# Attention followed by a mixture of adapters: the mixture steps of most batches placed one head pair later, and one batch's x transposed on TensorE

## The chip, the cores and the metric

The kernel runs on one core of a Trainium2 chip, in one launch. The metric is the device time in microseconds: 240.66 us is the median of 3 runs (239.62 to 241.18).

## The reference

Eight batches of T5-style attention (8 heads, 576 positions, 64 features a head), then a mixture of rank-16 adapters over all 4608 rows of 512 features. Shortened:

```
scores = q @ k.T / sqrt(64) + bias_table[bucket(|i - j|)]      # per batch and head
attn   = softmax(scores);  x = concat over heads of attn @ v   # x: 4608 x 512
logits = x @ w_gate                                            # 8 experts
w      = softmax over the two largest logits of a row
out    = x + sum over these two e of w_e * (x @ A[e]) @ B[e]
```

## The kernel before

All matmuls take bf16 operands. A **pair** is two heads of one batch; 8 batches of 4 pairs make 32 pairs, and a pair i has five steps g = 0 to 4, so n = 5 i + g counts 160 steps. In each step TensorE computes the scores of the next step (`qk(n + 1)`), ScalarE takes the exponential of this one (`expo(n)`, L350, 128x1024 elements), and VectorE multiplies the bias band into the one before (`band`). Steps 1 to 3 of a pair also multiply the probabilities of the pair before with v (`pv`, L380); VectorE divides by the row sums and so writes x (`recip`, `norm`). Step 0 transposes q and k of the next pair on TensorE (`transposes`, L297; copy kqT on VectorE). The first 512 positions of a batch go in tiles of 128; the last 64 positions of every two batches share one tile, the tail.

**The mixture** of batch b runs spread over the pairs of the batches behind it. The function `mixture(b)` puts each of its parts into the table `events` with `at_slot(di, g, ...)`: pair 4 (b + 1) + di, step g. The parts are, in the order in which they depend on one another: `m_xdma` (L432), a DMA that SyncE issues and that transposes the four 128-row tiles of x into xT, 16 blocks of 128x128, inside the core's memory; or `m_x`, which does the same with 16 transposes on TensorE into PSUM (two tiles `xps` of 8 blocks, L443) and two copies on VectorE, and which only the last batch uses; `m_xtail`, the tail's part of xT, for odd b; `m_logits` (L465), 16 or 20 matmuls from xT, a copy and the row maxima on VectorE, a subtraction on GpSimd; `m_gate`, an exponential on ScalarE and small operations on GpSimd and VectorE that make the gate; `m_z` (L511), 16 or 20 matmuls from xT, multiplied by the gate on VectorE; `m_zT`, transposes of z and a copy; `m_out` (L532, L542), for each of the four row tiles a matmul and an addition of x on VectorE, and after the second and the fourth tile four output stores that SyncE issues; `m_outt` (L547 to L557), the same for the tail.

**What sets the order.** The program is written out in order by hand. Every engine works through its own instructions in the order of the program and waits for what it needs; semaphores between engines come from the data. In one step the attention's parts are issued first and the step's `events` behind them. SyncE issues, in program order, the loads of q, k and v, the transpositions of x and the output stores; it is free to run ahead of the other engines until an instruction must wait. At step 0 of a batch's first pair stand the k and q loads of the next batch (`load_kq`, L106, 1 MB each) and eight loads of v (`load_v`, L114, 64 KB each); four more loads of v stand at step 0 of the second pair and four at step 0 of the third. GpSimd casts q, k (L147) and v (L152) to bf16 ahead of their use; the cast of v for a pair stands at the last step of the pair before it.

**Buffers.** x has four buffers, xT two, the loaded q, k and v two, the output tile o three. PSUM has two buffers for scores and four for all else (tag "acc").

Of the kernel before, what the change touches and what calls it, by code (L numbers as in the profile page):

```python
# [27 lines left out]
def kernel(  # L28
# [15 lines left out]
    B, H, S, D = q.shape  # L44
# [148 lines left out]
    for bv, lo, hi in runs[nsm:]:  # L193
        n = hi - lo
# [367 lines left out]
    def mixture(b):  # L562
        tail = b % 2 == 1
        i0 = HP * (b + 1)

        def at_slot(di, g, f, *a):
            events.setdefault(5 * (i0 + di) + g, []).append((f, a))

        if b < B - 1:
            at_slot(0, 4, m_xdma, b)  # L570
        else:
            at_slot(0, 4, m_x, b, 0)
            at_slot(0, 4, m_x, b, 1)
        if tail:
            at_slot(1, 4, m_xtail, b)
        at_slot(2, 0, m_logits, b)
        for n in range(4):
            at_slot(2, (2, 3, 4, 4)[n], m_gate, b, n)
        at_slot(3, 0, m_z, b, 0, 4)
        if tail:  # L580
            at_slot(3, 2, m_z, b, 4, 5)
        at_slot(3, 4, m_zT, b)
        at_slot(4, 0, m_out, b, 0)
        at_slot(4, 2, m_out, b, 1)
        at_slot(5, 0, m_out, b, 2)
        at_slot(5, 2, m_out, b, 3)
        if tail:
            at_slot(6, 4, m_outt, b)


    NPAIR = B * HP
# [1 line left out]
    for b in range(B):  # L593
        mixture(b)
    transposes(0)
    qk(0)
    for n in range(NG + 5):
        i, g = divmod(n, 5)
        b, hp = divmod(i, HP)
# [96 lines left out]
```

## Time and profile before

| | |
|---|---|
| median of 3 runs | 240.66 us (239.62 to 241.18) |
| profiled execution: span on the core, from the first to the last instruction | 235.5 us (its whole time is not given beside it) |
| TensorE busy | 178.6 us (76%), granted clock 0.915 on average |
| VectorE busy | 185.3 us (79%) |
| ScalarE busy | 160.7 us (68%), of it 153.3 us in the 160 exponentials |
| GpSimd busy | 101.2 us (43%) |
| DMA | 41.54 MB, mean 176 GB/s |

The profile is one execution. Busy times are sums over the whole span, with a start in which loads and the bias tables come in, and an end in which only the mixture of the last two batches is left. In it, L82 is a helper through which every VectorE instruction goes, so that VectorE's work is told apart by its tiles. PE is TensorE, PEld its weight load, DVE VectorE, ACT ScalarE, POOL GpSimd, SP SyncE; a q behind the name means the engine's queue (here: where it issues a DMA). PEclk is the granted share of TensorE's full clock.

### The profile page before, as it was taken

How to read it: one execution, taken by the hardware profiler on the slowest of the kernel's cores; microseconds unless marked ns; L12 is line 12 of the kernel's file. 1: busy time of each engine (PE TensorE's matmuls, PEld its weight loads, DVE VectorE, ACT ScalarE, POOL GpSimd, SP SyncE). 2: the span in 40 equal slices, each digit the busy share in tenths (PEclk: the TensorE clock that was granted, in tenths of full speed). 3: DMA queues.
4: the chain of work that ended last, by engine and by line, in shares of the span. 5: the costliest groups of instructions: out<-in, count | busy, mean ns of one | idle time of the engine just before them, and what ended most of it. 6: DMA issues, size and time to landing. Idle time of an engine off the chain costs nothing.

```text
span 235.5 us, 6536 instructions
## 1 busy us (share of the span) xinstructions
PE 178.6 (76%) x2485; PEld 120.5 (51%) x2496; DVE 185.3 (79%) x540; ACT 160.7 (68%) x180; POOL 101.2 (43%) x195
## 2 busy tenths in 40 slices
PE   0177749886999898869992799989892999986560
PEld 0034426554765665546661576566561766665420
DVE  6329648893999999949895389999993799998770
ACT  0368637994899799936993379988990789892000
POOL 8440797562455455534453144554551543220100
PEclk9998997997999999979997589999996799999957
DMA  6977999999978979964998899896998603810616
GB/s 170 197 177 209 346 154 213 260 143 183 330 95 171 190 206 268 207 146 83 268 190 186 182 263 202 184 180 124 332 153 188 133 0 85 187 42 8 180 38 185
DMA packets 91831, 41.54 MB, mean 176 GB/s; under 512 B 69648, under 2 KB 87192, under 8 KB 91800
## 3 DMA queue, kind: packets, MB, share of 16 engines
q1 hardware_dynamic: 71720, 38.75, 70.0%
q0 software_dynamic: 17888, 1.85, 15.4%
q10 hardware_dynamic: 2192, 0.53, 1.4%
q8 instruction: 19, 0.31, 0.6%
q14 instruction: 12, 0.10, 0.1%
HBM read 29.84 MB, written 9.45 MB: 167 GB/s over the span
## 4 chain that ended last, share of the span: by engine, by line
DVE 37%; PE 28%; DMA 20%; issue 4%; ACT 4%; SPq 2%; POOL 2%; POOLq 0%; DVEq 0%
DVE p L82 12%; DMA xT<-x 12%; PE pv L380 10%; DVE x L82 7%; PE sc L334 7%; DVE o L82 4%; ACT p L350 4%; DMA tl<-in_q_dram 2%; DVE rc L82 2%; DMA vf<-in_v_dram 2%; PE tps L306 2%; PE kqps L297 2%; DMA qf<-in_q_dram 2%; DVE kqT L82 2%; PE zp L511 2%
## 5 line engine op out<-in xcount | busy, mean ns | idle before, releaser
L350 ACT ACTIVATE p<-sc 128x1024 bf16<-128x1024 f32 x160 | 153.3, 1034 | 39.8 <-PE sc L334 30.7
L82 DVE TENSOR_TENSOR p<-p,M 128x512 bf16<-128x512 bf16 (+2 forms) x160 | 73.6, 475 | 0.0
L380 PE MATMUL pv<-vn,p 128*128 128x65 bf16 (+1 forms) x1152 | 62.7, 203 | 1.7 <-DVE p L82 1.7
L380 PEld LDWEIGHTS <-p 128*128 128x128 bf16 x1280 | 53.9, 102 | 12.1 <-issue 11.2
L334 PE MATMUL sc<-kqT 64*128 64x512 bf16 x256 | 52.7, 411 | 8.1 <-ACT p L350 5.2
L147 POOL CAST kqn<-qf 128x512 bf16<-128x512 f32 x29 | 17.8, 613 | 35.5 <-DVE rc L82 33.7
L297 PE MATMUL kqps<-ident,kqn 128*128 128x128 bf16 x256 | 21.6, 230 | 14.2 <-DVE kqn L82 7.9
L152 POOL CAST vn<-vf 128x512 bf16<-128x512 f32 x28 | 17.3, 620 | 30.8 <-DVE p L82 15.7
L380 PE MATMUL pv<-vt,p 128*128 128x130 bf16 x128 | 29.0, 227 | 0.0
L82 DVE COPY kqT<-kqps 128x1024 bf16<-128x1024 bf16 x32 | 21.9, 683 | 8.7 <-PE kqps L297 8.6
L297 PEld LDWEIGHTS <-kqn 128*128 128x128 bf16 x256 | 15.5, 102 | 23.0 <-DVE kqn L82 8.2
L334 PEld LDWEIGHTS <-kqT 64*128 64x128 bf16 x256 | 12.9, 94 | 24.2 <-issue 14.7
L82 DVE TENSOR_TENSOR o<-dl,x 128x512 f32<-128x512 f32 x32 | 21.4, 680 | 1.0 <-PE dl L532 0.7
L147 POOL CAST kqn<-kf 128x512 bf16<-128x512 f32 x29 | 18.0, 622 | 7.3 <-DVE p L82 6.3
L465 PE MATMUL lp<-Wb,xT 128*128 128x8 bf16 x144 | 5.1, 167 | 18.2 <-DMA xT<-x 17.0
L82 DVE TENSOR_TENSOR x<-pv,rc 128x384 bf16<-128x384 f32 x32 | 17.8, 557 | 1.1
L82 DVE RECIPROCAL rc<-pv 128x6 f32<-128x6 f32 x64 | 11.7, 182 | 4.3 <-PE pv L380 4.0
L465 PEld LDWEIGHTS <-xT 128*128 128x128 bf16 x144 | 4.4, 99 | 19.6 <-DMA xT<-x 18.1
L475 POOL TENSOR_TENSOR df<-lg,m 128x32 f32<-128x32 f32 (+1 forms) x8 | 2.1, 261 | 27.8 <-DVE m L82 27.8
L343 PEld LDWEIGHTS <-kqT 128*128 128x128 bf16 x128 | 10.2, 101 | 7.4 <-issue 3.0
L82 DVE COPY tlT<-tps 128x1024 bf16<-128x1024 bf16 x8 | 5.5, 690 | 10.3 <-PE tps L306 10.2
L82 DVE TENSOR_TENSOR x<-pv,rm 128x256 bf16<-128x256 f32 x32 | 13.3, 417 | 0.0
(79 smaller groups left out, 209.4 us busy)
## 6 DMA issues: line engine op xcount, KB each, us to landing
out_dram<-o SPq DMA_DIRECT2D x64, 128.0 KB, 2.4
vf<-in_v_dram SPq DMA_DIRECT2D x120, 64.0 KB, 3.9
kf<-in_k_dram SPq DMA_DIRECT2D x7, 1024.0 KB, 6.4
qf<-in_q_dram SPq DMA_DIRECT2D x7, 1024.0 KB, 10.5
kf<-in_k_dram SPq DMA_DIRECT2D x4, 256.0 KB, 3.2
qf<-in_q_dram SPq DMA_DIRECT2D x4, 256.0 KB, 3.7
out_dram<-ot SPq DMA_DIRECT2D x8, 128.0 KB, 2.3
vf<-in_v_dram ACTq DMA_DIRECT2D x8, 64.0 KB, 4.5
```

Of the source, the lines that this page charges most:

```text
L82: self.last = f(*a, **kw)
L147: return (eng or nc.gpsimd).tensor_copy(o, s)
L152: return (eng or nc.gpsimd).tensor_copy(vns[b % 2][:, :, h, :D], vfs[b][:, :, h, :])
L297: nc.tensor.transpose(o[:, :, j, :], n[:, w, j], ident)
L306: nc.tensor.transpose(ps[:, w, c, :], tls[b % 2][:, w, c, :], ident)
L334: nc.tensor.matmul(sc[:, h * 512:(h + 1) * 512], lhsT=t[s, 0, g * 128:(g + 1) * 128], rhs=t[s, 1, :], start=True, stop=True)
L343: nc.tensor.matmul(sc[:, o:o + 128], lhsT=t[:, 0, j * 128:(j + 1) * 128], rhs=tt[:, 1, hp, :], start=True, stop=True, skip_group_check=True)
L350: nc.scalar.activation(p, scs.pop(n), ACT.Exp, scale=scale)
L380: nc.tensor.matmul(acc[:, k, o:o + n], lhsT=lhsT, rhs=rhs, start=start, stop=stop, skip_group_check=True)
L465: nc.tensor.matmul(lp[:, t, :], lhsT=xT[:, 4 * t + c, :], rhs=Wb[:, c, :], start=first, stop=(c == 3), skip_group_check=True)
L475: nc.gpsimd.tensor_tensor(df, lg, m8[:, :, 0:1].to_broadcast((128, nt, E)), op=ALU.subtract)
L511: nc.tensor.matmul(zp[:, t - t0, :], lhsT=xT[:, 4 * t + c, :], rhs=Ab[:, c, :], start=(t == t0 and c == 0), stop=(c == 3), skip_group_chec ...
```

## The change

For batches 0 to 5 everything from `m_logits` on moves to one pair later (d = 3 in place of 2); the transposition by DMA and the tail's part of xT stay where they are. Batch 6 is transposed by `m_x` on TensorE, at the step where its DMA stood; its other parts, and all of batch 7, stay where they are. No function is new.

```diff
--- before.py
+++ after.py
@@ -566,26 +566,27 @@
         def at_slot(di, g, f, *a):
             events.setdefault(5 * (i0 + di) + g, []).append((f, a))
 
-        if b < B - 1:
+        if b < B - 2:
             at_slot(0, 4, m_xdma, b)
         else:
             at_slot(0, 4, m_x, b, 0)
             at_slot(0, 4, m_x, b, 1)
         if tail:
             at_slot(1, 4, m_xtail, b)
-        at_slot(2, 0, m_logits, b)
+        d = 3 if b < B - 2 else 2
+        at_slot(d, 0, m_logits, b)
         for n in range(4):
-            at_slot(2, (2, 3, 4, 4)[n], m_gate, b, n)
-        at_slot(3, 0, m_z, b, 0, 4)
+            at_slot(d, (2, 3, 4, 4)[n], m_gate, b, n)
+        at_slot(d + 1, 0, m_z, b, 0, 4)
         if tail:
-            at_slot(3, 2, m_z, b, 4, 5)
-        at_slot(3, 4, m_zT, b)
-        at_slot(4, 0, m_out, b, 0)
-        at_slot(4, 2, m_out, b, 1)
-        at_slot(5, 0, m_out, b, 2)
-        at_slot(5, 2, m_out, b, 3)
+            at_slot(d + 1, 2, m_z, b, 4, 5)
+        at_slot(d + 1, 4, m_zT, b)
+        at_slot(d + 2, 0, m_out, b, 0)
+        at_slot(d + 2, 2, m_out, b, 1)
+        at_slot(d + 3, 0, m_out, b, 2)
+        at_slot(d + 3, 2, m_out, b, 3)
         if tail:
-            at_slot(6, 4, m_outt, b)
+            at_slot(d + 4, 4, m_outt, b)
 
 
     NPAIR = B * HP
```

In a batch, with the first pair called 0: before, pair 0 had the first two outputs of the batch two before and, at step 4, the transposition; pair 1 the other two outputs; pair 2 the logits, the gate and, at step 4, the tail's output; pair 3 z and zT. After, pair 0 has z and zT and, at step 4, the transposition; pair 1 the first two outputs; pair 2 the other two; pair 3 the logits, the gate and, at step 4, the tail's output.

## Rows read from the trace of the kernel before

**Rows 1.** The page: chain that ended last, by line, shares of the span.
```profile
DVE p L82 12%; DMA xT<-x 12%; PE pv L380 10%; DVE x L82 7%; PE sc L334 7%; DVE o L82 4%; ACT p L350 4%; DMA tl<-in_q_dram 2%; DVE rc L82 2%; DMA vf<-in_v_dram 2%; PE tps L306 2%; PE kqps L297 2%; DMA qf<-in_q_dram 2%; DVE kqT L82 2%; PE zp L511 2%
```

**Rows 2.** Waits: engine, line <- releaser: us in total, times, longest us.
```profile
ACT p L350 <- PE sc L334: 30.7, 22, 6.3
PE lp L465 <- DMA xT<-x: 17.0, 6, 5.6
```

**Rows 3.** Timeline of ScalarE, batch 4: start, us, instructions, [idle before <- releaser].
```profile
132.17 1.02 ACT L350 ACTIVATE p<-sc 128x1024 bf16<-128x1024 f32 x1 [6.30 <-PE sc L334]
```

**Rows 4.** Stages: third pairs, batches 1 to 7. Length, busy by engine, clock, DMA.
```profile
core 0: us, PE busy (x) PEld busy (x) DVE busy (x) ACT busy (x) POOL busy (x), PEclk, DMA share, GB/s
51.70:60.64 8.94, 6.41 (x86) 4.47 (x86) 5.13 (x17) 5.12 (x8) 2.92 (x6) 0.81 0.94 192
76.09:82.70 6.61, 5.60 (x98) 4.04 (x97) 6.38 (x22) 4.92 (x8) 3.34 (x7) 1.00 0.97 182
98.38:108.00 9.62, 6.58 (x87) 4.81 (x87) 6.37 (x21) 5.02 (x7) 3.66 (x7) 0.82 0.80 149
123.94:137.70 13.76, 8.19 (x100) 5.93 (x98) 6.97 (x25) 5.13 (x7) 3.98 (x8) 0.63 0.85 186
153.01:158.90 5.89, 5.11 (x87) 3.71 (x87) 5.75 (x20) 5.02 (x7) 3.19 (x7) 1.00 0.96 181
174.94:186.78 11.84, 7.10 (x98) 5.05 (x97) 6.58 (x22) 5.03 (x8) 3.45 (x7) 0.71 0.82 175
202.46:208.13 5.67, 4.89 (x79) 3.44 (x80) 5.53 (x20) 4.91 (x8) 1.39 (x3) 1.00 0.47 113
```

**Rows 5.** Stages, same columns: batches 1, 5 and 7 whole.
```profile
42.09:65.86 23.77, 20.24 (x295) 14.00 (x295) 18.99 (x56) 19.51 (x24) 11.53 (x21) 0.93 1.25 222
...
142.71:164.61 21.90, 20.28 (x306) 13.70 (x306) 21.27 (x61) 19.79 (x24) 11.56 (x21) 1.00 0.88 161
...
192.16:213.20 21.04, 19.13 (x288) 12.84 (x288) 20.12 (x60) 19.67 (x23) 5.94 (x11) 1.00 0.39 89
```

**Rows 6.** Timeline of SyncE, its DMA issues around batch 4.
```profile
109.55 1.20 SPq L557 DMA_DIRECT2D out_dram<-ot  x2
110.85 0.53 SPq L106 DMA_DIRECT2D kf<-in_k_dram  x1
...
113.13 10.55 SPq L114 DMA_DIRECT2D vf<-in_v_dram  x8
123.78 2.21 SPq L542 DMA_DIRECT2D out_dram<-o  x4
126.10 2.58 SPq L432 DMA_TRANSPOSE xT<-x  x1
...
130.90 1.82 SPq L542 DMA_DIRECT2D out_dram<-o  x4
...
134.93 0.40 SPq L106 DMA_DIRECT2D kf<-in_k_dram  x1
...
164.84 8.42 SPq L114 DMA_DIRECT2D vf<-in_v_dram  x8
```

**Rows 7.** Tile xT, issue to landing; the chain in order of time, first transposition.
```profile
DMA to landing us min/median/max: 4.5/5.0/6.9
...
48.68 6.39 DMA xT<-x
```

**Rows 8.** Timeline of TensorE, logits in batch 7.
```profile
203.55 0.56 PE L465 MATMUL lp<-Wb,xT 128*128 128x8 bf16 x16
```

**Rows 9.** Groups by line, shapes apart: busy us, mean ns of one, idle before.
```profile
L443 PE MATMUL xps<-ident,x 128*128 128x128 bf16 x16 | 1.3, 220 | 0.5 <-DVE x L82 0.5
L82 DVE COPY xT<-xps 128x1024 bf16<-128x1024 bf16 x2 | 1.3, 680 | 0.0
```

**Rows 10.** Timeline, batch 7: scores of TensorE, x of VectorE.
```profile
197.21 0.39 PE L334 MATMUL sc<-kqT 64*128 64x512 bf16 x2
...
198.60 0.42 DVE L82 TENSOR_TENSOR x<-pv,rm 128x256 bf16<-128x256 f32 x1
```

## The prediction

> **What bounds the kernel now.** I began with the chain of waits, summed by line [rows 1]: the reader is to see that a single transfer, xT<-x, holds 12% of the span, as much as the costliest VectorE line. The view of waits says who pays [rows 2]: TensorE stood before its first logits matmul for 17.0 us in six waits, and ScalarE, whose exponentials are its main work, idled 30.7 us for the scores matmuls (qk). TensorE runs in order, so a logits matmul that waits for xT holds back the scores behind it. The timeline of ScalarE shows it at its worst [rows 3]: 6.30 us idle ahead of one exponential in batch 4.
>
> So I cut the run by head pairs (four to a batch; batches are 0 to 7 by their attention; a pair starts with its first exponential) and looked at the third pair of batches 1 to 7, where the logits of the batch before stand [rows 4]. They took 8.94, 6.61, 9.62, 13.76, 5.89, 11.84 and 5.67 us. In the long ones ScalarE and VectorE still have only 5.0 to 7.0 us of work, and the granted clock has fallen, to 0.63 in the worst, between its levels of 1.2 and 2.4 GHz, after TensorE stood idle; in the two short ones it is 1.00. I take 5.89 us as what the pair needs when nothing is late. The excess over it is 3.05 + 0.72 + 3.73 + 7.87 + 0 + 5.95 = 21.3 us. It holds the waits and the slow clock behind them: in batch 4, 7.87 us of excess came with 6.30 us of idle exponentials, a factor of 1.25, which I use below.
>
> A batch without a wait is bounded by VectorE: 21.27 us busy of 21.90 [rows 5], ScalarE 19.79. That is the floor: what the change can give back ends there.
>
> **Logits, gates, z, zT and outputs one pair later (batches 0 to 5).** The instructions stay the same in number; VectorE and ScalarE work is only moved between pairs of a batch that is full anyway, and the first batch loses as much of it as the last one gains: 0 us. What decides is whether xT has landed by the new place. The third wait-free pair ends 16.2 us after its batch starts [rows 4, 5], and the logits follow the next pair's start by about 1.1 us (203.55 against 202.46) [rows 4, 8]: needed at +17.3 us, against about 11.4 us before.
>
> Landing: the transposition takes 5.0 us from issue, between 4.5 and 6.9 [rows 7]. In batches 1 to 3 it has room: in batch 1 it landed at 55.1, 13.0 us after the batch's start [rows 5, 7], and nothing on SP in front of it moves later. Ahead of batch 3 the k and q loads stand behind output stores that move from a second to a third pair; even if these loads went out only at the batch's start, the stretch worked out below (11.9 us from k load to transposition) would land xT at +16.9. The waits there, 7.5 us of the excess, go.
>
> In batches 4 and 6 something on SP's queue does move: the store of the tail tile (ot) stands ahead of the next k and q loads. It now comes a pair later, and SP issues in order. Before, SP issued it 1.55 us after the fourth pair began (109.55 against 108.00) [rows 4, 6]. Now it will be about 1.6 us into the next batch. From there to the transposition SP spent 126.10 - 109.55 = 16.55 us [rows 6]; the four output stores between (2.3 us) move behind it, leaving 14.2 us. Of this 10.55 us are eight v loads, which took 8.42 us elsewhere [rows 6]; at the middle 13.2 us is left. Issue at +14.8, landing at +19.8, wanted at +17.3: a wait of 2.5 us in each of batches 4 and 6. Batch 5: SP goes from one transposition to the next k load in 134.93 - 126.10 = 8.83 us [rows 6], plus four stores of 1.9 us that come along: +25.5 us. With the wait, batch 4 lasts 21.9 + 3.1 = 25.0 us, so the load goes out 0.5 us into batch 5, the transposition 11.9 us later, and it lands at +17.4: no wait worth counting. Residual: 2 x 2.5 x 1.25 = 6.25 us. The bounds: nothing, if the v loads are quick and it lands in 4.5 us, up to the second rival's 12.9 us.
>
> The outputs stand one pair later too. By the code x of a batch b is last read in pair 4b+15 and its buffer written again in pair 4b+17, and an output tile's buffer comes round after 12 pairs: 0 us. With less lead for the loads, GpSimd's cast of v would be late next; its result is read more than a pair later, which covers some 5 us.
>
> **Batch 6 transposes on TensorE.** Removed: a DMA that nobody waited for, since the third pair of batch 7 is one of the two short ones. Added: 16 transposes and two copies of 0.68 us on VectorE. The same form is at the end of this kernel: 1.3 us busy on TensorE and 2 x 0.68 = 1.36 us on VectorE [rows 9]. There it ran in the drain; now it stands in a batch where VectorE is busy 20.12 of 21.04 us [rows 5], so 1.36 us are on the path. TensorE has finished the scores before it at 197.60 while the x it needs is written at 199.02 [rows 10], so it may also wait 1.42 us ahead of the next scores; of these 2.7 us TensorE's idle 1.9 us in that batch covers most. I take 1.6 us, ends 0 (all in gaps) and 2.8 us (1.36 + 1.42).
>
> The rows give 1.3 us for 16 transposes that overlap. The Trainium skill, "TensorE: Matmul & The Clock Gate", Part 4, gives some 275 ns for one in a kernel; 16 in a row would be an estimated 4.4 us by that page, 3.1 us more, and the time about 230. The trace disagrees: one lasts 219 ns and the group 1.3 us. The rows stay.
>
> **Sum.** 21.3 - 6.25 - 1.6 = 13.45 us less. The profiled span is 235.5 us, so 222.0; the median of the runs is 240.66 us, 5.2 us more than this span, and I keep that distance: **227.2 us**.
>
> **Rivals.**
> All waits vanish: the v loads go out in 8.4 us and xT lands in 4.5 us. For it: TensorE is never slowed, so nothing else is late; against: SP's issues follow one another almost without a break from 110.85 to 134.93 [rows 6], so it cannot run ahead. Saving 21.3 - 1.6 = 19.7: 221.0 us. Chance 0.17.
>
> The transposition queues behind the loads. It now stands straight behind eight v loads; the one transposition that already did so took 6.39 us [rows 7]. With slow v loads as well: issue +15.8, landing +22.2, waits 4.9, 0.5 and 4.9 us, x 1.25 = 12.9; saving 6.8: 233.8 us. Chance 0.19. The Trainium skill, "DMA: Bandwidth & Descriptors", section Queues, rings and completion order, says that each DMA engine takes the descriptors of a ring in order; by that rule this is what happens, and the 6.39 us agrees, though the longest, 6.9 us [rows 7], is another one.
>
> The wait only moves: loads and transpositions set the pace of batches 1 to 6, and each gains nothing, as when residual waits sum to 15 us or more. Time 240 to 242. For it: that stretch of SP is 24.1 us for a batch, longer than the 21.9 us floor. Against: a batch with batch 4's excess lasts 21.9 + 7.9 = 29.8 us, far above it. Chance 0.05.
>
> Slower: the k and q loads of the next batch, pushed behind the ot store, land after TensorE wants them. They are wanted with the fourth pair's transposes at +16.2; their landing lets the last v load go, at about +14.7, so the slack is 1.5 us less a cast. It decides once they need 6 us more than now: waits of 8.5, 6 and 8.5 us x 1.25 = 28.8, plus 1.6, less 21.3, 9 us lost: 250 us. Chance 0.04.
>
> **How the numbers follow.** The forecast, 0.55, stands for 224 to 230 us: residual waits of half to one and a half times mine. The range is from the first rival to the second, 220.8 to 233.8; beyond are part of the second rival and the last two. A measurement of this kernel tells 1% (2.4 us) from no change. Faster by more than that: 0.55 + 0.17 + 0.19 = 0.91; within: 0.05; slower: 0.04.
>
> **What would show it.** Third pairs of batches 1 to 6 at 5.0 to 6 us with a granted clock of 1.00. In batches 4 and 6 TensorE waits 1 to 4 us for xT at the start of the fourth pair, and SP issues the ot store 1 to 2 us into the batch; in 1 to 3 and 5 no wait over 1 us. In batch 7, 16 transposes with a wait for x ahead of them and a batch of 22 to 23 us. The prediction is wrong if xT waits stay in batches 1 to 3, if TensorE or GpSimd waits for k, q or v, or if the waits in 4 and 6 are gone.

## The result, and the profile after

The changed kernel takes 231.44 us (median of 4 runs, 230.42 to 236.33) against 240.14 us; the ratio, which leaves out the one disturbed run of 236.33, is 0.9688, with a 95% interval of 0.9592 to 0.9784. Measured again beside other kernels it took 230.24 us, ratio 0.9799 (0.9679 to 0.9918). The forecast was 227.2 us in a range of 220.8 to 233.8: direction and range held, the gain was 8.7 us where 13.45 were forecast. The profiled span fell from 235.5 to 228.9 us.

The chain of waits by line shows at once what happened (first line of it; it answers to [rows 1]):

```profile
DMA tl<-in_q_dram 15%; DVE p L82 11%; PE pv L380 6%; DVE x L82 6%; ACT p L350 6%; PE sc L334 4%; DVE o L82 4%; DVE kqT L82 3%; DVE rc L82 2%; DMA vf<-in_v_dram 2%; PE zp L511 2%; PE kqps L297 2%; DMA qf<-in_q_dram 2%; POOL kqn L147 2%; DVE zt L82 1%
```

The transfer xT<-x is gone from it, and another one, the load of the tail rows of q (tl), has taken its place and more. The list of waits of the changed kernel agrees (engine, line <- releaser: us in total, times, longest us; [rows 2]):

```profile
ACT p L350 <- PE sc L343: 11.7, 7, 3.1
PE tps L306 <- DMA tl<-in_q_dram: 11.4, 6, 3.2
ACT p L350 <- PE sc L334: 8.8, 8, 3.0
```

The 17.0 us that TensorE waited for xT are gone, and 11.4 us of waiting for the tail rows stand in the list. Of these, 3.2 us lie in batch 0, where the kernel before waited 3.5 us; new are the five waits in batches 1 and 3 to 6 (the list from 40 to 180 us):

```profile
PE tps L306 <- DMA tl<-in_q_dram: 8.3, 5, 2.5
```

ScalarE's 30.7 us behind the scores (with 7.1 us behind those of the fifth step, L343) have become 8.8 and 11.7. Cut by pairs as in [rows 4], the third pairs of batches 1 to 7 of the changed kernel:

```profile
core 0: us, PE busy (x) PEld busy (x) DVE busy (x) ACT busy (x) POOL busy (x), PEclk, DMA share, GB/s
53.07:59.17 6.10, 4.71 (x70) 3.19 (x70) 4.38 (x11) 4.79 (x6) 2.60 (x5) 1.00 1.23 129
75.28:80.71 5.43, 5.38 (x80) 3.63 (x79) 5.36 (x15) 4.91 (x6) 2.42 (x5) 1.00 1.02 203
97.74:104.70 6.96, 5.10 (x72) 3.31 (x72) 5.52 (x14) 4.68 (x6) 2.81 (x5) 1.00 1.22 183
121.34:128.77 7.43, 5.54 (x80) 3.64 (x79) 5.83 (x15) 4.90 (x6) 2.81 (x5) 1.00 1.34 183
145.41:151.91 6.50, 5.10 (x72) 3.31 (x72) 5.53 (x14) 4.69 (x6) 2.81 (x5) 1.00 1.01 143
168.54:176.61 8.07, 5.54 (x80) 3.65 (x79) 5.84 (x15) 4.91 (x7) 2.82 (x5) 1.00 1.17 194
194.64:200.90 6.26, 4.95 (x80) 3.43 (x80) 6.12 (x21) 4.91 (x7) 1.39 (x3) 1.00 0.33 88
```

Batches 1 to 6 sum to 40.5 us, where they were 56.7. The granted clock is 1.00 in all of them. But only batch 2's is at the 5.0 to 6 us that were forecast, although no logits are left in them. The timeline of TensorE in the third pair of batch 4 shows where the rest stands, and that the logits in the fourth pair no longer wait:

```profile
124.23 0.40 PE L306 MATMUL tps<-ident,tl 128*128 128x128 bf16 x4
126.47 0.38 PE L306 MATMUL tps<-ident,tl 128*128 128x128 bf16 x4 [1.85 <-DMA tl<-in_q_dram]
...
129.71 0.64 PE L465 MATMUL lp<-Wb,xT 128*128 128x8 bf16 x20
```

The first four tail transposes (k) run, the next four (q) wait 1.85 us. GpSimd issues the loads of these q rows at steps 1 and 3 of the second pair, and the transposes want them at step 2 of the third.

Why did this not show before? In batches 1 and 3 the wait for xT, in front of the tail transposes in the same pair, hid some of it: the second q load landed 13.4 and 14.4 us after the batch's start, and after the change TensorE asked for it at 12.5 and 14.1. In batches 4 to 6 there was nothing to hide. Before, that load landed at 12.4, 12.8 and 12.9 us; in batch 5, which waited 0.62 us for xT, the transposes came to it only at 14.1. After the change it lands at 16.2, 15.2 and 16.8 us, though it is issued at most 0.4 us later in the batch: it takes longer. The two q loads of batch 4, before and after:

```profile
DMA to landing us min/median/max: 2.4/3.2/4.0
DMA to landing us min/median/max: 5.8/6.4/7.0
```

With this goes a shift of SyncE's loads, which now run beside them: in batches 4, 5 and 6 the next k load goes out 2.9, 1.0 and 3.6 us after the batch's start, where it went out 2.9, 7.8 and 2.4 us ahead of it.

SyncE around batch 4 and batches 1, 5 and 7 as wholes, for [rows 6] and [rows 5]:

```profile
111.69 1.20 SPq L557 DMA_DIRECT2D out_dram<-ot  x2
112.99 0.54 SPq L106 DMA_DIRECT2D kf<-in_k_dram  x1
113.63 0.61 SPq L106 DMA_DIRECT2D qf<-in_q_dram  x1
114.33 8.20 SPq L114 DMA_DIRECT2D vf<-in_v_dram  x8
122.67 3.30 SPq L432 DMA_TRANSPOSE xT<-x  x1
```

```profile
43.47:64.26 20.79, 17.99 (x276) 12.21 (x276) 18.03 (x51) 19.21 (x24) 11.45 (x20) 1.00 1.22 213
...
134.31:157.35 23.04, 20.07 (x305) 14.00 (x307) 21.45 (x62) 19.59 (x23) 11.81 (x22) 1.00 0.98 216
...
182.15:205.79 23.64, 21.19 (x322) 14.96 (x323) 21.42 (x65) 19.97 (x23) 6.19 (x13) 1.00 0.30 79
```

The ot store goes out 1.55 us after batch 4 starts (110.14), as forecast (1.6). Batch 7 has grown by 2.6 us, from 21.04 to 23.64.

### The profile page after: what moved, and what is told of

The parts are those of the page before. It is cut to its first block, busy times and chain, and to the rows that moved or that the text cites. A ratio compares the mean times of both kernels' runs of the same rounds, so it can differ in the third digit from the quotient of the medians.

```text
span 228.9 us, 6562 instructions
## 1 busy us (share of the span) xinstructions
PE 174.3 (76%) x2502; PEld 118.0 (52%) x2512; DVE 186.4 (81%) x542; ACT 160.4 (70%) x180; POOL 102.2 (45%) x195
## 3 DMA queue, kind: packets, MB, share of 16 engines
q0 software_dynamic: 17888, 1.85, 16.2%
## 4 chain that ended last, share of the span: by engine, by line
DVE 38%; PE 20%; DMA 20%; issue 7%; ACT 6%; POOL 4%; SPq 2%; POOLq 0%; DVEq 0%; ACTq 0%
DMA tl<-in_q_dram 15%; DVE p L82 11%; PE pv L380 6%; DVE x L82 6%; ACT p L350 6%; PE sc L334 4%; DVE o L82 4%; DVE kqT L82 3%; DVE rc L82 2%; DMA vf<-in_v_dram 2%; PE zp L511 2%; PE kqps L297 2%; DMA qf<-in_q_dram 2%; POOL kqn L147 2%; DVE zt L82 1%
## 5 line engine op out<-in xcount | busy, mean ns | idle before, releaser
L350 ACT ACTIVATE p<-sc 128x1024 bf16<-128x1024 f32 x160 | 152.9, 1034 | 26.3 <-PE sc L343 11.7
L334 PE MATMUL sc<-kqT 64*128 64x512 bf16 x256 | 51.5, 399 | 12.4 <-ACT p L350 9.2
L380 PE MATMUL pv<-vn,p 128*128 128x65 bf16 (+1 forms) x1152 | 60.0, 199 | 0.0
L380 PEld LDWEIGHTS <-p 128*128 128x128 bf16 x1280 | 51.2, 99 | 11.2 <-issue 10.6
L297 PE MATMUL kqps<-ident,kqn 128*128 128x128 bf16 x256 | 21.3, 227 | 15.1 <-DVE kqn L82 7.4
L82 DVE COPY kqT<-kqps 128x1024 bf16<-128x1024 bf16 x32 | 21.9, 683 | 8.8 <-PE kqps L297 8.8
L380 PE MATMUL pv<-vt,p 128*128 128x130 bf16 x128 | 28.2, 220 | 0.0
L334 PEld LDWEIGHTS <-kqT 64*128 64x128 bf16 x256 | 13.5, 93 | 27.9 <-issue 18.7
L82 DVE TENSOR_TENSOR o<-dl,x 128x512 f32<-128x512 f32 x32 | 21.4, 681 | 1.0 <-PE dl L532 1.0
L82 DVE COPY tlT<-tps 128x1024 bf16<-128x1024 bf16 x8 | 5.5, 690 | 12.9 <-PE tps L306 12.9
L306 PE MATMUL tps<-ident,tl 128*128 128x128 bf16 x64 | 6.7, 241 | 11.4 <-DMA tl<-in_q_dram 11.4
L82 DVE RECIPROCAL rc<-pv 128x6 f32<-128x6 f32 x64 | 11.7, 182 | 3.7 <-PE pv L380 3.4
L343 PEld LDWEIGHTS <-kqT 128*128 128x128 bf16 x128 | 10.1, 100 | 7.7 <-issue 2.0
L339 PE MATMUL sc<-kqT,tlT 128*128 128x512 bf16 x32 | 12.6, 393 | 1.3 <-ACT p L350 1.0
L82 DVE TENSOR_TENSOR x<-pv,rm 128x256 bf16<-128x256 f32 x32 | 13.4, 418 | 0.0
L343 PE MATMUL sc<-tlT,kqT 128*128 128x128 bf16 x128 | 12.8, 225 | 0.0
```

The costliest lines, as they stand in the source:

```text
L82: self.last = f(*a, **kw)
L297: nc.tensor.transpose(o[:, :, j, :], n[:, w, j], ident)
L306: nc.tensor.transpose(ps[:, w, c, :], tls[b % 2][:, w, c, :], ident)
L334: nc.tensor.matmul(sc[:, h * 512:(h + 1) * 512], lhsT=t[s, 0, g * 128:(g + 1) * 128], rhs=t[s, 1, :], start=True, stop=True)
L339: nc.tensor.matmul(sc[:, 0:512], lhsT=tt[:, 0, hp, :], rhs=t[:, 1, :], start=True, stop=True)
L343: nc.tensor.matmul(sc[:, o:o + 128], lhsT=t[:, 0, j * 128:(j + 1) * 128], rhs=tt[:, 1, hp, :], start=True, stop=True, skip_group_check=True)
```

## The experiments

All ratios are to the kernel before, with 95% intervals. The runs came in three groups (e1 to e4, e5 to e8, e9 to e11), each on another chip with the kernel before beside it. The changed kernel itself came out at 0.9688 and 0.9799 in two measurements, so differences of some 1% between groups mean nothing.

**Each half of the change alone.** The later steps without the TensorE transposes:

```diff
-        if b < B - 2:
+        if b < B - 1:
             at_slot(0, 4, m_xdma, b)
```

> The later mixture steps alone; batch 6 keeps its transposition by DMA. If the later steps carry the whole gain and the TensorE transposes of batch 6 only cost, as forecast (1.6 us) or as batch 7 shows after the change (23.65 us against 21.04, so 2.6 us), this is 1.5 to 3 us faster than the changed kernel: 228 to 230 us, ratio to the kernel before about 0.953, batch 7 at 21 to 22 us. Rival: the seventh DMA transposition crowds the last loads, and it is no faster than the changed kernel (231.4 us).

Measured 229.66 us, ratio 0.9635 (0.957 to 0.970), batch 7 at 21.7 us. The later steps carry the whole gain; that they do better than the full change is not clear of noise, but batch 7 is shorter by 1.9 us than in the changed kernel's first profile (1.1 us than in its second, below). The tail rows are waited for here too, 2.35 and 3.10 us in batches 4 and 6.

The TensorE transposes without the later steps (kernel before, `if b < B - 2` ahead of `m_xdma`):

> Batch 6 transposed on TensorE alone; the mixture steps stay where they were. Forecast: 1.6 us slower than before (ends 0 and 2.8): 241.8 us, ratio 1.007, with TensorE waiting about 1.4 us for x ahead of the second eight transposes. Rival: the gaps of batch 7 take it and it is level, within 0.3%.

Measured 240.18 us, ratio 1.0093 (1.0048 to 1.0137): 0.93% of 238.55 us is 2.2 us lost (1.1 to 3.3), with 1.0 us of TensorE waiting for x in both places of such transposes together. The 1.6 us forecast lie inside; the transfer that they replace was waited for by nobody. In the profiled execution batch 7 is only 0.9 us longer than before (21.94 against 21.03).

**The wait for the tail rows.** The changed kernel with the q rows loaded beside those of k (and those of v, which follow them, a pair earlier too):

```diff
-        if g in (1, 3) and hp < 3 and nb < B:
-            load_tail(nb, hp, g // 2)
+        if g in (1, 3) and hp < 2 and nb < B:
+            for w in ((0, 1), (2,))[hp]:
+                load_tail(nb, w, g // 2)
```

> The changed kernel with the tail rows of q loaded one pair earlier, beside those of k. Theory A: after the change the tail transposes of the third pair wait for the tail rows of q (11.4 us in six waits, longest 3.2), and this wait was only hidden behind that for xT; with the rows there in time the six waits vanish and most of them is gained: 222 to 225 us, third pairs of batches 1 to 6 at 5.0 to 5.6 us. Rival B: the third pair is long because two outputs, the tail copy and the sums meet on VectorE in it; the waits vanish, the pairs stay above 6 us and the time is 229 to 231. Rival C, the residual wait of the forecast: with shorter third pairs xT is late in batches 4 and 6, waits of 1 to 3 us at the fourth pair come back, and the time is 225 to 228.

Measured 226.11 us, ratio 0.9433 (0.9352 to 0.9514): faster than the later steps alone in the same group (0.9635), in the direction of A. The time is that of rival C, and so is the profile (of the longest of the six executions): the third pairs of batches 1 to 6 fall to 33.7 us in sum, 5.15 to 6.08 each, so rival B finds little support, and TensorE waits for xT in the fourth pairs of batches 4 and 6 again, 2.50 and 2.13 us.

The same edit in the kernel before:

> The kernel before with the tail rows of q loaded one pair earlier and nothing else. Theory A: before the change the wait for xT stood first in the third pair and hid the tail rows of q completely, so nothing is gained: 240 us, ratio 0.997 to 1.003. Rival B: the same, as the wait never mattered. If it is faster by more than 1 us, the tail rows already cost time before, and the page's list of waits (3.5 us, one wait, in the first batch) missed them.

Measured 244.42 us, ratio 1.0267 (1.0192 to 1.0342). No theory had this: it is slower. The waits say how; TensorE stands longer for xT (17.0 us before):

```profile
PE lp L465 <- DMA xT<-x: 21.5, 6, 5.7
```

The transpositions took a median of 5.4 us to land, with 7.5 us the longest (5.0 and 6.9 before).

So I left the loads alone and moved what waits for them: the tail transposes one pair later.

```diff
-        if g == 2 and hp == 2 and nb < B:
+        if g == 2 and hp == 3 and nb < B:
             tail_transposes(nb)
```

> The changed kernel with the tail transposes one pair later (fourth pair), all loads where they were. Theory A (the third pair waits for the tail rows of q): those waits vanish without any change to a transfer; third pairs of batches 1 to 6 fall from 5.4 to 8.1 us to 5.0 to 5.5, and xT becomes late in batches 4 and 6, as with the earlier loads, by 2 to 3 us each: 224 to 226 us, ratio 0.94. Rival B (VectorE fills the third pair): third pairs keep 6 us and more, 229 to 231 us.

Measured 227.94 us, ratio 0.9531 (0.9453 to 0.9608), against 0.9688 and 0.9799 for the changed kernel. No wait for the tail rows is left in batches 1 to 6, and their third pairs take 4.56, 4.98, 4.70, 4.98, 4.70 and 4.98 us, 28.9 in sum against 40.5. Of the 11.6 us between them 8.3 are the waits of these batches; the rest is mostly work that left the pair, the transposes and the copy of them: batch 2, which waited for nothing, fell from 5.43 to 4.98 us. Rival B falls: VectorE did not fill the third pair. But xT is late again in batches 4 and 6, in the fourth pair, as the forecast had it for the change itself. The stretches of the fourth pairs of batches 4 and 6 (same columns as above), SyncE's issues around batch 4, which starts at 103.88, and TensorE's logits:

```profile
120.12:129.87 9.75, 6.68 (x90) 4.78 (x90) 6.68 (x24) 5.03 (x8) 3.04 (x6) 0.82 0.84 173
168.16:177.48 9.32, 6.68 (x90) 4.79 (x90) 6.67 (x24) 5.04 (x7) 3.04 (x6) 0.82 0.83 181
```

```profile
106.03 1.20 SPq L557 DMA_DIRECT2D out_dram<-ot  x2
107.33 0.55 SPq L106 DMA_DIRECT2D kf<-in_k_dram  x1
107.98 0.61 SPq L106 DMA_DIRECT2D qf<-in_q_dram  x1
108.68 9.66 SPq L114 DMA_DIRECT2D vf<-in_v_dram  x8
118.66 1.84 SPq L432 DMA_TRANSPOSE xT<-x  x1
```

```profile
124.09 0.65 PE L465 MATMUL lp<-Wb,xT 128*128 128x8 bf16 x20 [2.87 <-DMA xT<-x]
```

The transposition is issued 14.8 us after the batch's start; the forecast said 14.8. The waits are 2.87 and 2.45 us (forecast 2.5 each), and the two pairs stand 4.1 and 3.6 us over the 5.7 us of a fourth pair without it, 7.7 us for a forecast of 6.25.

The same move in the kernel before:

> The kernel before with the tail transposes one pair later and nothing else. Theory A: the wait for the tail rows was hidden behind the wait for xT, so moving the transposes gives nothing: 238 to 241 us, ratio 0.99 to 1.005. It also tells whether the slower time with earlier tail loads (ratio 1.027) comes from the loads: here they are not moved, so it must not be slower by more than 1%; if it is, the place of the transposes is the reason.

Measured 239.08 us, ratio 0.9977 (0.9925 to 1.0029): nothing, as A said: before the change the place of the tail transposes cost no time, because the rows were there or xT was waited for longer. Why the earlier loads of the fourth experiment cost 2.7% stays open. The longer landing does not show it: here, with all loads in their old places and no slowdown, xT also takes a median of 5.4 us (longest 6.7), and TensorE waits 17.6 us for it.

**The ot store.** On top of the later tail transposes, the store of the tail output in a part of its own, `m_outt_store`, one step behind the next loads:

```diff
             at_slot(d + 4, 4, m_outt, b)
+            at_slot(d + 5, 0, m_outt_store, b)
```

> As the one before, and the store of the tail output is issued behind the next batch's k, q and first v loads instead of ahead of them. If that store is what makes xT late in batches 4 and 6 (the step of the forecast), their waits at the fourth pair vanish and another 4 to 7 us is gained: 218 to 221 us, ratio 0.915. Rival: SyncE and the transfers are full, the loads then push the transposition by as much, and the time stays within 1% of the kernel before it in this list.

Measured 224.0 us, ratio 0.9412 (0.9349 to 0.9475). The waits in batches 4 and 6 are gone: their fourth pairs take 5.78 us each. In batch 4 the k load goes out 1.4 us ahead of the batch's start (103.03) instead of 3.4 us behind it (first fence), and the two tail loads of q, issued where they were, land sooner (second fence: with the store ahead of the loads, then behind them):

```profile
101.61 1.29 SPq L106 DMA_DIRECT2D kf<-in_k_dram  x1
103.00 0.53 SPq L106 DMA_DIRECT2D qf<-in_q_dram  x1
103.62 9.77 SPq L114 DMA_DIRECT2D vf<-in_v_dram  x8
113.73 1.28 SPq L561 DMA_DIRECT2D out_dram<-ot  x2
115.12 3.18 SPq L432 DMA_TRANSPOSE xT<-x  x1
```

```profile
DMA to landing us min/median/max: 6.0/6.8/7.5
DMA to landing us min/median/max: 2.4/3.3/4.2
```

But of the 7.7 us that stood in these two pairs 5.0 came back in a new wait in batch 5, where none had been: 2.81 us for xT, and the pair at 10.74 us with a granted clock of 0.68:

```profile
140.89:151.63 10.74, 7.78 (x87) 5.51 (x87) 6.68 (x23) 5.12 (x7) 2.98 (x6) 0.68 1.06 190
```

From k load to k load SyncE now needs 22.4, 25.2 and 23.2 us (79.20, 101.61, 126.83, 150.07), more than the 21.4 to 21.8 us of a batch without a wait: it may have become the pace, which the third rival of the forecast expected of the changed kernel; this is argued from the issue times and not shown alone. Against the later tail transposes alone the time falls by 1.2%, between what was expected and the rival. The same with batch 6 by DMA:

> The later mixture steps, batch 6 by DMA, tail transposes one pair later and the tail store behind the loads. If the TensorE transposes of batch 6 cost 2.2 us here too (0.93% when made alone), this is 1 to 3 us faster than the same kernel with them: 216 to 219 us, ratio 0.905. Rival: the DMA transposition of batch 6 falls into the last loads and its logits, which stand one pair later now, still have it in time either way: level within 0.5%.

Measured 222.6 us, ratio 0.9379 (0.9317 to 0.9440), the lowest median of all runs, and not told apart from the one above: not the 216 to 219 us expected, but the rival. With the store behind the loads here too, TensorE waits for xT in batch 4 again, and 0.96 us in batch 6; the next k load went out 1.8 us after the start of batch 4:

```profile
124.58 0.65 PE L465 MATMUL lp<-Wb,xT 128*128 128x8 bf16 x20 [3.00 <-DMA xT<-x]
```

So the wait for xT wanders between the batches of these two kernels, and the place of the ot store is not all of its cause.

**The v loads.** Is it their place in front of the transposition that makes xT late? On top of the later tail transposes, with the ot store where the change put it, the first eight of a batch go behind it:

```diff
-            for j in ((0, 1), (2,), (3,), ())[hp]:
+            for j in ((), (0, 1, 2), (3,), ())[hp]:
                 load_v(nb, (j,))
```

The changed kernel unaltered, beside these:

> The changed kernel itself, unaltered, beside the two that follow. Theory A: 231.4 us or a ratio near 0.969 as first measured, tail-row waits of about 11 us in six waits. If its ratio lies under 0.955, the gain of 4 to 7 us put down to the tail rows was drift between chips.

Measured 230.24 us, ratio 0.9799, tail waits of 10.3 us in six, 4.2 of them in batch 0: the same picture, but for one wait for xT, 1.58 us in the fourth pair of batch 5.

> The changed kernel with the tail transposes one pair later, and the first eight v loads of a batch issued behind the transposition of x instead of ahead of it; the tail store stays where the change put it. If xT is late in batches 4 and 6 because SyncE reaches it only after these loads (issue at 14.8 us after the batch's start), it is now issued once x is written, 7 to 9 us after the start, and lands at 12 to 14 us, ahead of the logits at 17.3: no wait for xT in any batch, 219 to 222 us, ratio 0.92 to 0.93, against 0.953 with the loads ahead. Rival: SyncE's loads set the pace; then v comes late, the casts of v on GpSimd wait, and the time is within 1% of that kernel.

Measured 230.77 us, ratio 0.9807 (0.9664 to 0.9951): level with the unaltered kernel beside it, so the gain of the later tail transposes is lost. What happens is the rival's mechanism, but the time is worse than its "within 1%" of 0.953. Straight behind the k and q loads the transposition lands no earlier (in batch 4, 21.0 us after the batch's start; 20.2 with the loads ahead); SyncE stands at it for 6.55 us, and it lands after a median of 9.3 us. v comes late, and GpSimd's casts wait:

```profile
112.39 6.55 SPq L432 DMA_TRANSPOSE xT<-x  x1
```

```profile
DMA to landing us min/median/max: 5.9/9.3/11.8
```

```profile
POOL vn L152 <- DMA vf<-in_v_dram: 9.9, 3, 4.4
```

On top of the kernel with the later steps, DMA for batch 6, the later tail transposes and the store behind the loads:

> As the kernel with later steps, DMA for batch 6, later tail transposes and the tail store behind the loads, and now the first eight v loads behind the transposition too. The one xT wait that was left (about 3 us and a slow clock behind it) should go: 217 to 220 us, ratio 0.915 to 0.925. Rival: loads pace it, within 0.5% of 0.938.

Measured 230.11 us, ratio 0.9767 (0.9589 to 0.9946), with 8.5 us of casts waiting for v: v late again, and more lost than the rival's "within 0.5% of 0.938".

## Why the prediction was right in direction and too large in size

Span by stages, before to after, each from the starts of the first exponentials of the pairs:

| stage | forecast | measured |
|---|---|---|
| third pairs, batches 1 to 6 | -21.3 | 56.7 to 40.5: -16.2 |
| fourth pairs, batches 1 to 6 | +6.25 | 32.4 to 33.0: +0.6 |
| first and second pairs, batches 1 to 6 | 0 | 61.0 to 65.2: +4.2 |
| batch 7 | +1.6 | +2.6 |
| end behind the last exponential | 0 | 22.3 to 23.1: +0.8 |
| start, up to batch 1 | 0 | 42.1 to 43.5: +1.4 |
| sum | -13.45 | -6.6 |

Two errors cancel in part: the forecast left out 8.3 us of waits in the third pairs, and it expected 6.25 us in the fourth pairs that did not come. That the time lies inside the range is to that extent luck. Two of its own signs of being wrong did appear: TensorE waits for q (its tail rows), and the waits in batches 4 and 6 are gone.

**What bounds it: right.** The wait for xT was on the path in the third pair. It went, with the low clock behind it, in all six batches of the first profile, and the later steps alone give the whole gain.

**The step that failed** is "I take 5.89 us as what the pair needs when nothing is late". It asked what the pair costs without the wait for xT, and not what TensorE meets next in the same pair; and where the forecast moved SyncE's loads later in the batch, it followed this to xT, to k and q and to the cast of v, and put the tail rows at nothing. The tail transposes wait for them 8.3 us in five of the six batches, shown by moving only the transposes (these waits go, and the third pairs fall from 40.5 to 28.9 us with the work that leaves them; 0.9531). Of this, some 1 to 2 us in batches 1 and 3 had been hidden before (an estimate from the landings above). The 5.5 us in batches 4 to 6 are new: the rows land there 2.4 to 3.9 us later in the batch than before, and sooner again in the kernel whose ot store, behind the loads, lets these out before the batch starts. That the other loads slow them fits all the profiles, but was not tried alone.

**Work moved within a full batch: 0 us, right for a batch.** The first and second pairs grew by 4.2 us, and the third shrank by some 3.4 us beyond its waits (an estimate: without a wait it takes 5.15 to 5.43 us in the kernels with the later steps, against the 5.89 of the forecast, in which TensorE waited 0.62 us for xT). With the tail wait out of the way batches 2, 3 and 5 take 21.78, 21.44 and 21.81 us, at the forecast floor of 21.9.

**The residual wait in batches 4 and 6: right in its place and its size, but not in this kernel, and its cause only in part.** The eight v loads of batch 4 took 8.20 us, less than at any place read before. Still xT landed at 18.7 and 19.2 us after the start of batches 4 and 6, later than the 17.3 at which it was wanted; the tail wait held TensorE up ahead of the logits for longer. Without the tail wait the residual appeared, 2.87 and 2.45 us. With the ot store behind the loads it vanished in both batches in one kernel, which got a wait of 2.81 us in batch 5 instead, and stood at 3.00 us in batch 4 in the other.

**Batch 6 on TensorE: a cost, its size open.** 1.6 us forecast, 2.2 us (1.1 to 3.3) measured alone, where the profile shows batch 7 longer by 0.9. In the changed kernel batch 7 grew by 2.6 us, in its second profile by 1.8; its first pairs now hold z and zT of batch 5 as well, and with the later steps alone it grew by 0.7. Between the last two kernels with the ot store behind the loads, one with the transposes on TensorE and one with the DMA, no difference is seen (22.77 and 22.78 us in batch 7). Half of the bound of 2.8 us was the wait for x; in the changed kernel it was 0.69 us:

```profile
188.25 1.00 PE L443 MATMUL xps<-ident,x 128*128 128x128 bf16 x15
189.94 0.23 PE L443 MATMUL xps<-ident,x 128*128 128x128 bf16 x1 [0.69 <-DVE x L82]
```

**Around the span.** Every run with both numbers shows 1.8 us between device time and span (230.69 and 228.9 in the changed kernel). The 5.2 us that I kept joined the span of one execution with the median of others; the profiled execution of before must itself have taken about 237.3 us by that (an estimate), below the medians of the kernel before beside the later runs (238.55, 239.29 and 238.56). Set against that execution, the forecast span of 222.0 us was missed by 6.9 us, not by 4.2.

**Rivals.** The transposition that queues behind loads did not happen in the changed kernel (landing 4.3 to 6.2 us), but did when it stood straight behind the k and q loads (9.3 us). "The wait only moves" may have named the pace-maker of the kernels that came later. The end's 0.8 us stand in every kernel with the later steps (22.7 to 23.1 us against 22.3 to 22.4); that it is the ot copy of batch 5, now in the last step, is likely and was not tried. The start differs from run to run (39.4 to 44.1 us) and does not follow the change. What SyncE's 22 to 25 us for a batch are made of, and so whether the last wait can go, stays open.

## What to carry to other kernels

Before you credit the removal of a wait, list what the same engine does next in that stretch, and for each input write down when it lands without the wait: the second-latest input sets what you gain. A list of waits names only the latest one; nothing that stood behind it has a row. And where one queue issues loads, stores and transpositions in order, moving a store means moving every load behind it: read the landings of all transfers that then run at the same time again, those of other queues too, and do not take them from the profile before.

## What the runs showed of the hardware that was not expected

A transposing DMA of 512 KB held SyncE's queue for 1.8 to 4.0 us in the usual order of the loads, with landings of 4.4 to 5.9 us (medians of the runs), and for 3.1 to 7.7 us straight behind 2 MB of k and q loads, with medians of 8.4 and 9.3 us in those two runs. The 32 KB loads of the tail's q rows, issued by GpSimd, took 2.4 to 4.1 us to land in batches 4 to 6 before the change, and 4.8 to 7.0 us after it, when SyncE's loads went out 5.7 to 8.8 us later in the batch. Four loads of 32 KB a batch brought forward by one pair cost the kernel before 2.7%. And the length of TensorE's wait did not tell whether the granted clock fell: over the third pair of batch 6 in the changed kernel it stayed at 1.00 with a wait of 2.48 us, and over that of batch 4 with the later steps alone it was 0.84 with one of 2.35 us.
